# Softmax denominators of an attention stage moved from VectorE to GpSimd

## The chip, the core and the metric

The kernel runs on one core of a Trainium2 chip. Its engines are TensorE (PE in the profile; its weight loads are shown as PEld), VectorE (DVE), ScalarE (ACT), GpSimd (POOL) and SyncE (SP, which issues nearly all DMAs here). Each engine works through its own queue in program order and waits on semaphores for the others. The metric is the time of one execution on the device, in microseconds, as the median of several runs.

## The reference

Three networks follow one another. Chunked attention on q, k and v of 4 x 8 x 576 x 64 (chunks of 64 rows), then a mixture of 8 experts on 2304 x 512 whose shares are made doubly stochastic by 8 Sinkhorn rounds, then a dense layer with a softmax-gated activation and a layer norm.

```python
scores = scale * np.matmul(q_c, k_c.transpose(0, 1, 2, 4, 3))
scores = scores - np.max(scores, axis=-1, keepdims=True)
attn = np.exp(scores)
attn = attn / (np.sum(attn, axis=-1, keepdims=True) + 1e-09)   # the change is here
out = np.matmul(attn, v_c)
...
logits = x @ w_gate
P = np.exp(logits - logits.max())
for _ in range(8):
    P /= P.sum(1, keepdims=True) + 1e-09
    P /= P.sum(0, keepdims=True) + 1e-09
    P *= N / E
for e in range(E):
    h = np.maximum(x @ w1[e], 0.0)
    out += P[:, e:e + 1] * (h @ w2[e])
...
ln = (solu - mu) / np.sqrt(var + 1e-06) * g_ln
return ln @ w_out
```

## The kernel before, in words

The order of all instructions is written out by hand (a manual schedule), and every engine keeps to it.

**Attention.** 2304 rows are 18 tiles of 128 (two chunks of 64 rows each); a tile holds all 8 heads. A loop over s = 0 to 23 runs five stages of different tiles in each step, in this order: `attn_exp(s - 3)`, `attn_pv(s - 6)`, `attn_pt(s - 5)`, `attn_qk(s - 2)`, `attn_t(s)`. `attn_t` transposes q or k on PE (L196) and copies the result (ACT L201, DVE L203). `attn_qk` makes the scores (PE L214), their maxima (DVE L227) and subtracts them (DVE L228) into a tile `p` of 128x512. `attn_exp` exponentiates `p` on ACT (L240), sums each head on DVE (L241) into `sm`, 128x8, adds 1e-9 (DVE L242), takes the reciprocal (DVE L243), and multiplies `p` by it on GpSimd (L244). `attn_pt` transposes the multiplied `p` on PE (L252) two steps later, and ACT copies it (L256). `attn_pv` multiplies by v (PE L267) and copies to `xf` (ACT L279, DVE L281).

**What is woven into the same steps.** Every three tiles make a half pass of x. For the products in three passes x and the weights are split in a rounded high part (ACT, L297 for x, L150 for weights) and a low part (`split`: L151, `x_lo`: L301), and the low parts are GpSimd's here. For a Strassen-like scheme sums of blocks of x (`x_sums`, L332) and of weights (L543 to L548) are made, also on GpSimd. `run_side` and `run_w` pop such pieces from two queues once in a step, behind the attention stages. Low parts of x that are needed again later are stored to DRAM by SP (L303), and the buffer is then free for another block. From s = 18 on the first products of the experts (`l1`) are run in the steps, and for each half pass the gate's products (`gate`, PE L352), whose logits go into the Sinkhorn rounds (L380 to L421).

**After attention.** The Sinkhorn steps run beside the first expert's products; from about 200 us on the kernel is a long sequence of expert products (L663, L803, L854), and the last layer follows with a power of -0.5 on GpSimd (L1051) in each of its 18 tiles.

The change touches `attn_exp` (L237 to L246) and two places where constants are made (L140 and L1098).

Of the kernel before, what the change touches and what calls it, by code (L numbers as in the profile page):

```python
# [9 lines left out]
F32 = mybir.dt.float32  # L10
# [3 lines left out]
ALU = mybir.AluOpType  # L14
# [30 lines left out]
def chunk_attention_sinkhorn_moe_solu_kernel(  # L45
# [13 lines left out]
    nc = tc.nc  # L59
    P = 128  # L60
# [11 lines left out]
    EPS = 1e-9  # L72
# [30 lines left out]
    const = ctx.enter_context(tc.tile_pool(name="const", bufs=1))  # L103
# [34 lines left out]
    ident = const.tile([P, P], F32, name="ident")  # L138
    ones = const.tile([P, P], F32, name="ones")
    mhalf = const.tile([P, 1], F32, name="mhalf")  # L140
    g_sb = const.tile([P, KF], F32, name="g_sb")
    wg_raw = const.tile([P, KD, E], F32, name="wg_raw")

# [92 lines left out]
    def attn_exp(t):  # L236
        p, sm = attn[t]  # L237
        flat = p.rearrange("p a h x -> p (a h x)")
        heads = p.rearrange("p a h x -> p (a h) x")
        nc.scalar.activation(out=flat, in_=flat, func=AF.Exp, scale=SCALE)  # L240
        nc.vector.tensor_reduce(out=sm, in_=heads, axis=AX.X, op=ALU.add)  # L241
        nc.vector.tensor_scalar(out=sm, in0=sm, scalar1=EPS, scalar2=None, op0=ALU.add)  # L242
        nc.vector.reciprocal(out=sm, in_=sm)  # L243
        nc.gpsimd.tensor_tensor(  # L244
            out=heads, in0=heads, in1=sm.unsqueeze(2).to_broadcast([P, H, 64]), op=ALU.mult
        )  # L246
# [844 lines left out]
    with tc.manual_schedule():  # L1091
# [4 lines left out]
            nc.tensor.transpose(warm[:, :P], ident, ident)  # L1096
        nc.gpsimd.memset(ones, 1.0)
        nc.gpsimd.memset(mhalf, -0.5)  # L1098
        nc.gpsimd.memset(wg.bitcast(F32), 0.0)

        def split_gate():
# [45 lines left out]
        for s in range(NT + 6):  # L1147
# [20 lines left out]
            if 0 <= s - 3 < NT:  # L1168
                attn_exp(s - 3)
# [190 lines left out]
```

## Time and profile before

| | us |
|---|---|
| median of 3 runs | 1817.55 (1816.68 to 1820.86) |
| the profiled execution, its own time | 1817.96 |
| its span, first to last instruction | 1816.2 |
| PE busy | 1761.7 |
| DVE busy | 1468.2 |
| GpSimd busy | 1050.5 |
| ACT busy | 612.7 |

The rows of the profile name a line of the kernel (L244), an engine, an operation, the tile written and the tiles read (`p<-p,sm`, without buffer numbers), and the shape as partitions x elements. Times are counted from the start of the span. An idle time in square brackets stands in front of an instruction, with what ended it. A line can be a helper's: L151 and L301 are the low parts of many tiles. Where instructions of one engine overlap a little in the timeline, the next one had begun while the last was draining.

### The profile page before, as it was taken

What the parts mean: (1) busy time and instruction counts of PE and PEld (TensorE: products, weight loads), DVE (VectorE), ACT (ScalarE), POOL (GpSimd) and SP (SyncE); (2) the same over time, 40 slices, a digit from 0 to 9 for tenths busy, and PEclk for the clock granted to TensorE, in tenths of its full rate; (3) what the DMA queues carried; (4) which work ended last, traced back from release to release, by engine and by line L of the source; (5) the groups of instructions that cost most, each with busy time, mean ns of one, the idle gap of its engine ahead of it and who ended that gap; (6) DMA issues with size and microseconds to landing.
All of it is one profiled execution on the core that took longest, in us unless ns stands there. A gap on an engine that the chain in (4) does not pass through costs nothing.

```text
span 1816.2 us, 31895 instructions
## 1 busy us (share of the span) xinstructions
PE 1761.7 (97%) x10827; PEld 1701.4 (94%) x10827; DVE 1468.2 (81%) x2264; ACT 612.7 (34%) x1368; POOL 1050.5 (58%) x1111
## 2 busy tenths in 40 slices
PE   6889999999999999999999999999999999999999
PEld 5678999999999999999999999899999999988887
DVE  6858899999888867778788888988888877766664
ACT  6743344444444312222232222222222322222222
POOL 3776799999988415445466666566565666400000
PEclk9999999999999999999999999999999999999999
DMA  7684887988978897998987989888889878842110
GB/s 187 186 292 173 283 280 289 335 317 290 316 280 312 312 346 276 336 351 307 326 300 263 313 280 389 294 283 280 280 285 286 270 255 278 293 148 64 56 47 30
DMA packets 313443, 476.21 MB, mean 262 GB/s; under 512 B 47664, under 2 KB 116416, under 8 KB 313280
## 3 DMA queue, kind: packets, MB, share of 16 engines
q1 hardware_dynamic: 312848, 471.80, 76.0%
q8 instruction: 87, 1.43, 0.3%
q10 hardware_dynamic: 432, 2.36, 0.3%
q14 instruction: 76, 0.62, 0.1%
HBM read 323.51 MB, written 150.54 MB: 261 GB/s over the span
## 4 chain that ended last, share of the span: by engine, by line
PE 79%; DMA 5%; DVE 5%; issue 2%; POOL 1%; SPq 0%; ACT 0%; POOLq 0%; DVEq 0%; ACTq 0%
PE y L803 18%; PE y L854 17%; PE Y L663 14%; PE X L663 9%; PE Z L663 9%; PE po L1077 5%; PE mh L1020 5%; DMA wl_A<-wk 3%; PE lt L1065 1%; DMA wk<-w_S 1%; DMA x_B<-xk_B 1%; DVE acc L830 1%; DVE c L733 0%; POOL w_A L151 0%; DVE h L738 0%
## 5 line engine op out<-in xcount | busy, mean ns | idle before, releaser
L803 PE MATMUL y<-h,w_A 128*128 128x384 f32 x1536 | 305.7, 336 | 6.9 <-DVE acc L830 3.9
L683 POOL TENSOR_TENSOR ho_T<-hT,ho_T 128x384 fp32r<-128x384 f32 x188 | 210.6, 1122 | 174.4 <-ACT ho_T L682 166.9
L803 PEld LDWEIGHTS y<-h,w_A 128*128 128x128 f32 x1536 | 269.9, 188 | 10.1 <-ACT w_S L609 3.2
L151 POOL TENSOR_TENSOR w_A<-raw,w_A 128x256 fp32r<-128x256 f32 x224 | 191.7, 869 | 73.5 <-ACT w_A L150 51.1
L758 DVE TENSOR_TENSOR t<-Y,s 128x384 f32<-128x384 f32 x192 | 106.1, 552 | 112.7 <-PE Y L663 95.7
L830 DVE TENSOR_TENSOR acc<-y,acc 128x768 f32<-128x768 f32 (+1 forms) x192 | 175.6, 915 | 9.5 <-PE y L803 8.5
L854 PE MATMUL y<-ho_T,wl_S 128*128 128x384 f32 x864 | 172.8, 335 | 0.9 <-DVE acc L872 0.5
L874 DVE TENSOR_TENSOR acc<-y,acc 128x768 f32<-128x768 f32 (+1 forms) x165 | 150.5, 915 | 17.9 <-PE y L854 17.9
L803 PE MATMUL y<-h,wl_A 128*128 128x384 f32 x768 | 153.7, 337 | 3.3 <-DMA wl_A<-wk 3.3
L663 PE MATMUL Y<-x_T,wl_S 128*128 128x384 f32 x768 | 153.8, 334 | 0.0
L663 PE MATMUL X<-x_B,wl_A 128*128 128x384 f32 x768 | 153.7, 334 | 0.0
L854 PEld LDWEIGHTS y<-ho_T,wl_S 128*128 128x128 f32 x864 | 151.6, 188 | 2.1 <-DVE acc L872 0.8
L737 ACT ACTIVATE h<-c 128x384 fp32r<-128x384 f32 x132 | 69.2, 525 | 237.0 <-DVE c L733 228.4
L803 PEld LDWEIGHTS y<-h,wl_A 128*128 128x128 f32 x768 | 136.0, 190 | 4.8 <-ACT w_S L609 1.8
L682 ACT ACTIVATE ho_T<-hT 128x384 fp32r<-128x384 f32 x192 | 99.0, 516 | 108.4 <-POOL hT L691 103.5
L682 ACT ACTIVATE ho_B<-c 128x384 fp32r<-128x384 f32 x96 | 50.5, 526 | 251.7 <-DVE c L716 206.9
L663 PEld LDWEIGHTS Y<-x_T,wl_S 128*128 128x128 f32 x768 | 135.0, 188 | 0.0
L663 PEld LDWEIGHTS X<-x_B,wl_A 128*128 128x128 f32 x768 | 135.0, 188 | 0.0
L1051 POOL TENSOR_TENSOR r<-r,mhalf 128x1 f32<-128x1 f32 x18 | 9.9, 550 | 208.3 <-DVE r L1048 208.3
L758 DVE TENSOR_TENSOR c<-Z,t 128x384 f32<-128x384 f32 x192 | 105.0, 547 | 19.6 <-PE Z L663 12.7
L151 POOL TENSOR_TENSOR w_S<-ws,w_S 128x256 fp32r<-128x256 f32 x128 | 110.3, 880 | 9.3 <-ACT w_S L150 8.2
L854 PE MATMUL y<-ho_B,wl_A 128*128 128x384 f32 x576 | 114.8, 334 | 0.0
(172 smaller groups left out, 3871.6 us busy)
## 6 DMA issues: line engine op xcount, KB each, us to landing
wl_S<-wk SPq DMA_DIRECT2D x448, 256.0 KB, 5.2
wl_A<-wk SPq DMA_DIRECT2D x400, 256.0 KB, 5.2
wk<-w_S SPq DMA_DIRECT2D x256, 256.0 KB, 5.1
wk<-w_A SPq DMA_DIRECT2D x208, 256.0 KB, 4.4
raw<-in_moe_w_dram SPq DMA_DIRECT2D x77, 512.0 KB, 5.9
sh<-spread SPq DMA_DIRECT2D x64, 192.0 KB, 8.1
kept<-wp SPq DMA_DIRECT2D x32, 256.0 KB, 4.6
xk_T<-x_T SPq DMA_DIRECT2D x8, 768.0 KB, 4.8
```

Source lines behind the costliest of these rows:

```text
L151: (eng or nc.vector).tensor_tensor(out=lo, in0=src, in1=hi.bitcast(F32), op=ALU.subtract)
L663: nc.tensor.matmul(b, w[:, a, kk, :], x[:, c, kk, :], start=(first and kk == 0 and n == 0), stop=(kk == 1 and n == 2), skip_group_check=no ...
L682: nc.scalar.activation(out=hi, in_=x, func=AF.Copy)
L683: f = lambda: eng.tensor_tensor(out=lo, in0=x, in1=hi.bitcast(F32), op=ALU.subtract)
L737: nc.scalar.activation(out=hi, in_=hp, func=AF.Copy)
L758: nc.vector.tensor_tensor(out=c_of[n], in0=bank_, in1=c_of[other], op=ALU.add)
L803: nc.tensor.matmul(y, wo2[u, f"A{d // 2 + 1}{f + 1}"][:, a, i * P:(i + 1) * P], h[:, c, f, :], start=(f == 0 and n == 0), stop=(f == 1 and ...
L830: nc.vector.tensor_tensor(out=at, in0=y, in1=at, op=ALU.add)
L854: nc.tensor.matmul(y, wo2[unit(m + q_)[1], wn][:, a, i * P:(i + 1) * P], hop[m // 2, bn][:, q_, c, :], start=(q_ == 0 and o == 0), stop=(q ...
L874: nc.vector.tensor_tensor(out=at, in0=y, in1=at, op=ALU.add)
L1020: nc.tensor.matmul(ph[:, n * 512:(n + 1) * 512], x[a][:, kk, :], m_in[kk, c][:, n * 512:(n + 1) * 512], start=(kk == 0 and i == 0), stop=( ...
L1077: nc.tensor.matmul(po[t], lt[f // 4][a][:, f % 4, :], m_out[f, c], start=(f == 0 and i == 0), stop=(f == KF - 1 and i == 2),)
```

## The change

The addition of 1e-9 and the reciprocal, both on DVE, become an addition and a power of -1 on GpSimd, ahead of the multiplication that was already there. The power takes its exponent from a constant tile of 128x8, filled once at the start by GpSimd.

```diff
@@ -138,6 +138,7 @@
     ident = const.tile([P, P], F32, name="ident")
     ones = const.tile([P, P], F32, name="ones")
     mhalf = const.tile([P, 1], F32, name="mhalf")
+    mone = const.tile([P, 8], F32, name="mone")
     g_sb = const.tile([P, KF], F32, name="g_sb")
     wg_raw = const.tile([P, KD, E], F32, name="wg_raw")
 
@@ -239,8 +240,8 @@
         heads = p.rearrange("p a h x -> p (a h) x")
         nc.scalar.activation(out=flat, in_=flat, func=AF.Exp, scale=SCALE)
         nc.vector.tensor_reduce(out=sm, in_=heads, axis=AX.X, op=ALU.add)
-        nc.vector.tensor_scalar(out=sm, in0=sm, scalar1=EPS, scalar2=None, op0=ALU.add)
-        nc.vector.reciprocal(out=sm, in_=sm)
+        nc.gpsimd.tensor_scalar(out=sm, in0=sm, scalar1=EPS, scalar2=None, op0=ALU.add)
+        nc.gpsimd.tensor_tensor(out=sm, in0=sm, in1=mone, op=ALU.pow)
         nc.gpsimd.tensor_tensor(
             out=heads, in0=heads, in1=sm.unsqueeze(2).to_broadcast([P, H, 64]), op=ALU.mult
         )
@@ -1096,6 +1097,7 @@
             nc.tensor.transpose(warm[:, :P], ident, ident)
         nc.gpsimd.memset(ones, 1.0)
         nc.gpsimd.memset(mhalf, -0.5)
+        nc.gpsimd.memset(mone, -1.0)
         nc.gpsimd.memset(wg.bitcast(F32), 0.0)
```

## Rows read from the trace of the kernel before

**Rows 1.** The page, section 1: busy us, share of the span, instructions.

```profile
PE 1761.7 (97%) x10827; PEld 1701.4 (94%) x10827; DVE 1468.2 (81%) x2264; ACT 612.7 (34%) x1368; POOL 1050.5 (58%) x1111
```

**Rows 2.** Busy by stretch: us, PE, PEld, DVE, ACT, POOL busy, PEclk, DMA, GB/s.

```profile
14.00:56.08 42.08, 33.06 (x587) 28.04 (x587) 35.08 (x65) 28.44 (x51) 17.19 (x17) 0.88 0.70 168
56.08:106.65 50.57, 40.18 (x719) 34.44 (x717) 42.37 (x71) 38.48 (x70) 44.70 (x36) 0.97 0.71 204
106.65:200.00 93.35, 81.82 (x474) 76.17 (x470) 66.48 (x156) 33.88 (x88) 59.31 (x78) 0.96 0.67 240
200.00:1816.20 1616.20, 1597.39 (x8948) 1554.94 (x8947) 1319.64 (x1969) 504.49 (x1150) 928.18 (x972) 1.00 0.77 268
```

**Rows 3.** Grouped lines, 0 to 190 us: count | busy us, mean ns | idle before.

```profile
L244 POOL TENSOR_TENSOR p<-p,sm 128x512 f32<-128x512 f32 x18 | 18.8, 1042 | 31.0 <-DVE sm L243 17.8 <-ACT kt L201 13.1
...
L241 DVE TENSOR_REDUCE sm<-p 128x8 f32<-128x512 f32 x18 | 12.3, 686 | 7.9 <-ACT p L240 7.6
...
L242 DVE TENSOR_SCALAR sm<-sm 128x8 f32<-128x8 f32 x18 | 9.6, 532 | 0.6
...
L243 DVE RECIPROCAL sm<-sm 128x8 f32<-128x8 f32 x18 | 3.6, 203 | 0.6
```

**Rows 4.** Instructions of tile sm: duration ns min/median/max, first and last start.

```profile
L242 DVE TENSOR_SCALAR sm<-sm x18: 171/208/1648, 14.2 to 99.6; 128x8 f32<-128x8 f32 x18
```

**Rows 5.** Timeline, DVE and GpSimd near 58 us: start us, us.

```profile
56.08 3.59 POOL L301 TENSOR_TENSOR x_B<-xf,x_B 128x768 fp32r<-128x768 f32 x2 [1.37 <-ACT x_B L297]
...
58.38 1.31 DVE L242 TENSOR_SCALAR sm<-sm 128x8 f32<-128x8 f32 x1
```

**Rows 6.** Grouped lines of DVE, 56.08 to 102 us.

```profile
L242 DVE TENSOR_SCALAR sm<-sm 128x8 f32<-128x8 f32 x9 | 7.4, 822 | 0.3
```

**Rows 7.** Busy by stretch, GpSimd alone: us, POOL busy, PEclk, DMA, GB/s.

```profile
56.08:82.42 26.34, 26.26 (x20) 0.94 0.76 209
82.42:106.65 24.23, 18.44 (x17) 1.00 0.65 199
```

**Rows 8.** Instructions of line 1051, in the last layer.

```profile
L1051 POOL TENSOR_TENSOR r<-r,mhalf x18: 549/549/554, 1608.3 to 1802.1; 128x1 f32<-128x1 f32 x18
```

**Rows 9.** Grouped lines of GpSimd, 56.08 to 106.6 us.

```profile
L301 POOL TENSOR_TENSOR x_B<-xf,x_B 128x768 fp32r<-128x768 f32 x8 | 14.5, 1824 | 3.9 <-ACT x_B L297 3.7 <-DMA v<-in_v_dram 0.2
...
L151 POOL TENSOR_TENSOR w_S<-ws,w_S 128x256 fp32r<-128x256 f32 x4 | 2.9, 722 | 0.0
```

**Rows 10.** Timeline: two GpSimd sums, the second reading the first's result.

```profile
94.77 0.74 POOL L543 TENSOR_TENSOR ws<-raw,raw 128x256 f32<-128x256 f32 x1
...
95.58 0.74 POOL L544 TENSOR_TENSOR ws<-ws,raw 128x256 f32<-128x256 f32 x1
```

**Rows 11.** Timeline, 73 to 88 us: GpSimd's results and who uses them.

```profile
73.68 1.81 POOL L332 TENSOR_TENSOR xs_T<-xf 128x768 f32<-128x768 f32 x1
...
75.82 1.58 ACT L297 ACTIVATE x_T<-xs_T 128x768 fp32r<-128x768 f32 x2
...
81.39 1.03 POOL L244 TENSOR_TENSOR p<-p,sm 128x512 f32<-128x512 f32 x1
...
87.64 0.66 PE L252 MATMUL pt<-ident,p 128*128 128x128 f32 x4
```

**Rows 12.** Timeline, 103 to 117 us: the last splits on GpSimd and what follows.

```profile
103.03 3.62 POOL L301 TENSOR_TENSOR x_B<-xf,x_B 128x768 fp32r<-128x768 f32 x2 [0.15 <-DMA v<-in_v_dram]
...
105.54 1.47 SPq L303 DMA_DIRECT2D xk_B<-x_B  x2
...
107.19 1.64 PE L352 MATMUL pg<-x_B,wg 128*128 128x384 f32 x8
...
113.62 0.85 ACT L297 ACTIVATE x_B<-xf 128x768 fp32r<-128x768 f32 x1 [2.04 <-DMA xk_B<-x_B]
...
115.44 0.84 ACT L297 ACTIVATE x_B<-xf 128x768 fp32r<-128x768 f32 x1 [0.97 <-DMA xk_B<-x_B]
...
116.64 0.61 PE L803 MATMUL y<-h,w_A 128*128 128x384 f32 x2 [2.08 <-ACT w_A L150]
```

## The prediction, made before the changed kernel was run

> **What bounds the kernel now.** I read the page's busy line first [rows 1]: PE has work in 97% of the span, so time can be won or lost only where PE stands still. The table by stretch [rows 2] says where: from 200 us to the end PE is busy 1597.4 of 1616.2 us, while from 14 to 56.08 us it has 33.1 of 42.1, from 56.08 to 106.65 us 40.2 of 50.6, and from 106.65 to 200 us 81.8 of 93.4. The change touches only attention, whose 18 tiles run in the first two of these stretches. What follows is a fixed sequence of products on an in-order PE, so a shift of attention's end goes to the end of the kernel nearly whole. The question is what paces attention from 56.08 to 106.65 us. There DVE is busy 42.4 of 50.6 us and GpSimd 44.7, ACT 38.5 [rows 2]. DVE and GpSimd are both near their limit, and the change moves work from one to the other.
>
> **What DVE is rid of.** The grouped lines [rows 3] give per tile the sum L241 0.69 us, the addition L242 0.53 us in the mean, the reciprocal L243 0.20 us, and on GpSimd the multiplication L244 1.04 us. The addition's own work is 0.17 us, its shortest; the longest took 1.65 us [rows 4]. The long ones are waits inside the instruction: the addition that starts at 58.38 us lasts 1.31 us, to 59.69 us, and GpSimd's pair of splits that starts at 56.08 us and lasts 3.59 us ends at 59.67 us [rows 5]. So this addition stands until GpSimd's running instruction is over. In the 18 tiles that is 9.6 - 18 x 0.17 = 6.5 us [rows 3, 4], of which 7.4 - 9 x 0.17 = 5.9 us lie in the nine tiles after 56.08 us [rows 6]. With both instructions gone DVE saves 0.17 + 0.20 and two gaps of some 0.03 us, about 0.44 us a tile, or 8 us, and 6.5 us of waiting: 14.5 us in all. That is a ceiling for a gain, reached only if DVE alone paced the stage.
>
> **What GpSimd gets.** Each tile's multiplication is preceded by an addition and a power on 128x8, and both must be through before it. GpSimd runs in order, so behind them stand, in this stage, the splits of x and of the weights and the sums of x. Before 56.08 us GpSimd has 24.9 us free of 42.1 [rows 2], and most of the additional work disappears there. After it there is no room: from 56.08 to 82.42 us GpSimd is busy 26.26 of 26.34 us, and from 82.42 to 106.65 us 18.44 of 24.23 us [rows 7]. It has 0.08 + 5.79 = 5.9 us free in the whole stretch.
>
> The power's price is the unknown. The only row is the same operation on one column, 0.549 us, without spread [rows 8]. A simple instruction costs less: a split of 256 columns takes 0.722 us and one of 768 columns 1.824 us [rows 9], so 2.15 ns a column and 0.17 us for the instruction. Of the power's 0.549 us some 0.38 us are therefore its own, and the trace doesn't say whether they come once or with every column. Once: 0.55 + 7 x 0.002, about 0.56 us for eight columns. With every column: 0.17 + 8 x 0.38 = 3.2 us. Below 0.55 us it can't come, eight columns being no less work than one. I take 1.3 us, the geometric middle, which is nearer to the row: that is about a quarter of the 0.38 us for each further column. The addition is 0.17 + 8 x 0.00215 = 0.19 us. Then an instruction that needs the one before it starts late: 94.77 + 0.74 = 95.51 us, and the next at 95.58 us [rows 10], 0.07 us; there are two such links, 0.14 us. (The new memset at the start is one small instruction where GpSimd only waits for the first sums: nothing.) So a tile costs GpSimd 0.19 + 0.14 + 1.3 = 1.63 us more, 0.88 us at the low end and 3.53 us at the high end.
>
> GpSimd's row for the one column can be set beside a rule. The Trainium skill, "GPSIMD Engine Reference", section 4.1 "Engine selection", says not to put ordinary elementwise work on this engine, about twice as slow as VectorE for two inputs and about line rate for one. By it an estimate of the power would be 2 x 0.203 = 0.41 us, the tile's sum 0.74 us and the shift below 9 x 0.74 - 7.4 = -0.7 us, no change. The row of 0.549 us for a single column is already dearer, so I don't take it.
>
> **The sum.** In the stretch after 56.08 us lie nine tiles: 9 x 1.63 = 14.7 us more for GpSimd. Its 5.9 us of free time take some of it, since the late engine finds its inputs ready. And the stretch can begin earlier, by what DVE's relief before 56.08 us makes of it: nothing at least, 9 x 0.44 + 0.6 = 4.6 us at most; I take 1.5 us, since DVE is busy only 35.1 of 42.1 us there [rows 2] and the loads of q, k and v also set the pace. GpSimd's last split of the stretch then ends 14.7 - 5.9 - 1.5 = 7.3 us later than at 106.65 us.
>
> Is this lateness covered? A tile's multiplication is consumed two steps later: the one that ends at 82.42 us by the transposes at 87.64 us [rows 11], some 5 us of slack. That hides the first tiles. But GpSimd's delay is 1.63 us more with every tile, and by the fifth it is past the slack. ACT is caught sooner: the sum of x that ends on GpSimd at 73.68 + 1.81 = 75.49 us is copied by ACT at 75.82 us [rows 11], 0.3 us later, and ACT is in order; three tiles lie before it, 3 x 1.63 - 1.5 = 3.4 us of delay, and the exponentials and copies of attention wait behind that copy. So DVE's relief after 56.08 us is given back, since its inputs come late.
>
> At the end of the stretch there is no slack either [rows 12]. GpSimd's two splits end at 103.03 + 3.62 = 106.65 us, and PE's gate products start at 107.19 us. The same splits are stored by SP from 105.54 us, and ACT waits for those stores at 113.62 us (2.04 us idle) and at 115.44 us. After the second it copies the weights, for which PE waits 2.08 us at 116.64 us. A split that is 7 us late makes this whole chain 7 us late, and with it the last gate, the Sinkhorn steps and the first expert's products.
>
> The profiled execution has a span of 1816.2 us and took 1817.96 us, 0.4 us above the median of 1817.55 us; its sums hold for the median as they stand. 1817.55 + 7.3 = 1824.9 us: I predict 1825 us.
>
> **The rivals.** (1) The power costs little more than for one column. At 0.56 us the tile has 0.88 us and the shift is 9 x 0.88 - 5.9 - 1.5 = 0.5 us: 1818 us, no change. It holds up to a power of about 0.9 us, where 9 x 1.23 - 7.4 = 3.7 us. For it speaks that columns of simple instructions are cheap [rows 9]; against it that 0.38 us for a single column is more than any fixed cost that the rows show. The rule of the Trainium skill named above ends here too.
>
> (2) DVE paces the stage and GpSimd's lateness stays within the two steps of slack. Then its 14.5 us come off, until ACT, busy 38.5 of 50.6 us, is the next limit: I put half, 7 us, so 1810.5 us. It decides where the tile's additional cost on GpSimd falls below what its free time and the earlier start give, (5.9 + 1.5) / 9 = 0.8 us a tile. With the low end of the one and the ceiling of the other it is 9 x 0.88 - 5.9 - 4.6 = -2.6 us; the 7 us need, besides, that the late splits and sums are not what the stage waits for. For it speak the 5.9 us of waiting in the addition; against it that GpSimd has no free time from 56.08 to 82.42 us [rows 7].
>
> (3) The power is paid with every column, 3.2 us. Then GpSimd is full from the first tile on: 17.19 + 44.70 us [rows 2] and 18 x 3.53 = 63.5 us make 125.4 us in a stretch of 92.65 us, 32.8 us more: 1850 us.
>
> **How the numbers follow.** The forecast, a power between 0.9 and about 2.6 us, has 0.55; (3) and its neighbourhood 0.10; (1), together with a lateness that is made good after 106.65 us, where GpSimd has 34 us free [rows 2], 0.25; (2) 0.10. A measurement of this kernel can tell 0.2%, 3.6 us, from no change. So slower has 0.65, the same 0.25, faster 0.10. The range leaves out most of (2) and the far end of (3): 1815 to 1846 us. At a power of 2.6 us the shift is 9 x 2.93 - 7.4 = 19 us, so the forecast's own range is 1821 to 1837 us.
>
> **What would show it.** On the profile after: the duration of the power on 128x8, between 0.56 and 3.2 us, is the step on which all hangs. DVE should have lost both instructions, and the 6.5 us of waiting with them. GpSimd should be busy without a gap from about 55 us to the last split of attention, and that split should end some 7 us after 106.65 us, with ACT waiting for GpSimd's sums of x and PE for the multiplied tiles, where before neither did. The gap between that split and the start of the steady products should stay. I am wrong if GpSimd still has gaps in that stretch, if the transposes come earlier in spite of a later GpSimd, or if a late split is made good before 200 us.

## The result, and the profile after

The changed kernel takes 1830.76 us (median of 4 runs, 1829.84 to 1831.3) beside 1819.2 us of the kernel before (4 runs, 1816.68 to 1821.8): ratio 1.0073, interval 1.0056 to 1.0091. The two medians lie 11.6 us apart, and by the ratio it is about 13 us slower. Its profiled execution has a span of 1829.0 us, 12.8 us more than before. Nearly all of it, 12.1 us, has arisen by the end of the Sinkhorn rounds. The page's busy line of after, to be set beside [rows 1]:

```profile
PE 1767.0 (97%) x10827; PEld 1706.4 (93%) x10827; DVE 1458.2 (80%) x2228; ACT 613.5 (34%) x1368; POOL 1085.0 (59%) x1148
```

GpSimd has 34.5 us more, and 18 tiles times the two new instructions are 18 x (0.243 + 1.667) = 34.4 us. These are their durations (instructions of tile sm in after: duration ns min/median/max, first and last start):

```profile
L243 POOL TENSOR_SCALAR sm<-sm x18: 238/243/245, 16.1 to 116.8; 128x8 f32<-128x8 f32 x18
L244 POOL TENSOR_TENSOR sm<-sm,mone x18: 1665/1667/1682, 16.5 to 117.1; 128x8 f32<-128x8 f32 x18
L245 POOL TENSOR_TENSOR p<-p,sm x18: 1041/1042/1044, 18.2 to 118.8; 128x512 f32<-128x512 f32 x18
```

On DVE the reciprocal of the same 128x8 took 0.203 us [rows 3]: here the move made an operation eight times as long. The Trainium skill, "GPSIMD Engine Reference", section 4.1 "Engine selection", puts an elementwise addition, multiplication or maximum of two inputs at about twice VectorE's time there; the section names no power. The trace shows that it can't be carried over to one: the power took 1.667 us, where twice the DVE row of the reciprocal is 0.41 us.

The table by stretch of after (us, then busy time of PE, PEld, DVE, ACT, POOL, PEclk, DMA, GB/s), to be set beside [rows 2]:

```profile
14.00:56.08 42.08, 34.19 (x588) 28.26 (x584) 31.61 (x47) 30.03 (x53) 31.41 (x32) 0.89 0.73 168
56.08:106.65 50.57, 35.39 (x651) 30.12 (x650) 30.88 (x47) 33.65 (x60) 48.60 (x42) 0.90 0.61 175
106.65:120.00 13.35, 7.50 (x58) 6.20 (x58) 1.18 (x3) 4.15 (x9) 12.78 (x14) 0.74 0.48 146
```

In the second row DVE, ACT and PE all do less than before in the same 50.57 us (30.88, 33.65 and 35.39 us; before 42.37, 38.48 and 40.18), and GpSimd alone is full. From 106.65 to 120 us DVE has 1.18 us of work and GpSimd 12.78 of 13.35. PE's granted clock is lower as well, 0.90 in the second row instead of 0.97, but that can't have made GpSimd late, for GpSimd never stood for PE there. Its timeline shows it, with the stretch's first pair of splits, one tile, and the last pair:

```profile
38.54 0.73 POOL L544 TENSOR_TENSOR ws<-raw,raw 128x256 f32<-128x256 f32 x1 [3.60 <-DMA v<-in_v_dram]
...
59.15 3.60 POOL L302 TENSOR_TENSOR x_B<-xf,x_B 128x768 fp32r<-128x768 f32 x2
62.70 0.74 POOL L152 TENSOR_TENSOR w_S<-ws,w_S 128x256 fp32r<-128x256 f32 x1
63.53 0.24 POOL L243 TENSOR_SCALAR sm<-sm 128x8 f32<-128x8 f32 x1
63.85 1.67 POOL L244 TENSOR_TENSOR sm<-sm,mone 128x8 f32<-128x8 f32 x1
65.60 1.04 POOL L245 TENSOR_TENSOR p<-p,sm 128x512 f32<-128x512 f32 x1
...
119.85 3.62 POOL L302 TENSOR_TENSOR x_B<-xf,x_B 128x768 fp32r<-128x768 f32 x2
```

None of its lines from 38.54 to 119.85 us carries a bracket, those left out here included, except the first: no idle time of note. From the start of the addition to the start of the multiplication it is 65.60 - 63.53 = 2.07 us (2.08 in most tiles). The first pair begins at 59.15 us where before it was 56.08 us [rows 5], the last at 119.85 us where it was 103.03 us [rows 12]. So the stretch is 60.70 us instead of 46.95 us, 13.75 us longer, and it began 3.07 us later.

What waited for GpSimd, directly or behind another engine, from 56 to 118 us of after (engine, line and releaser: us in total, times, longest):

```profile
PE px L268 <- ACT qt L202: 9.6, 3, 4.5
PE pg L353 <- POOL x_B L302: 6.1, 2, 5.5
PE pt L253 <- POOL p L245: 2.8, 3, 1.7
...
ACT lt L361 <- PE pg L353: 11.2, 3, 8.3
ACT x_T L298 <- POOL xs_T L333: 9.9, 4, 4.3
...
DVE sm L242 <- ACT p L241: 16.1, 6, 6.3
```

PE's waits for splits and multiplied tiles, and ACT's for sums of x, are new. ACT stands 9.9 us for the sums, and 11.2 us for the gate's products (before, 4.1 us), 8.3 us of them in one piece behind the 5.5 us for which PE stands for a split. Behind ACT DVE stands for the exponentials, 16.1 us: more than the addition, its waiting and the reciprocal had cost it. At the end DVE stands for the last multiplied tile itself (waits of after from 118 us on; this one had begun earlier):

```profile
DVE xf L282 <- POOL p L245: 12.3, 1, 12.3
```

The lateness goes on to the end of attention (timeline of SP: the DMA that spreads the Sinkhorn result, first of before, then of after):

```profile
176.76 0.87 SPq L444 DMA_DIRECT2D spread<-pws  x2
```

```profile
188.89 0.88 SPq L445 DMA_DIRECT2D spread<-pws  x2
```

It comes 12.1 us later, and the last layer's first product comes at 1604.85 instead of 1592.04 us, 12.8 us later. So 16.8 us at the last split are 12.1 us at the spread, and what is late there stays late.

### The profile page after: what moved, and what is told of

It is laid out like the page before. It is cut to its first block, busy times and chain, and to the rows that moved or that the text cites. A ratio compares the mean times of both kernels' runs of the same rounds, so it can differ in the third digit from the quotient of the medians.

```text
span 1829.0 us, 31896 instructions
## 1 busy us (share of the span) xinstructions
PE 1767.0 (97%) x10827; PEld 1706.4 (93%) x10827; DVE 1458.2 (80%) x2228; ACT 613.5 (34%) x1368; POOL 1085.0 (59%) x1148
## 4 chain that ended last, share of the span: by engine, by line
PE 80%; DVE 5%; DMA 4%; POOL 2%; issue 2%; SPq 0%; ACT 0%; POOLq 0%; DVEq 0%; ACTq 0%
PE y L804 18%; PE y L855 18%; PE Y L664 15%; PE X L664 10%; PE Z L664 9%; PE po L1078 5%; PE mh L1021 5%; DMA wl_A<-wk 2%; DMA wk<-w_S 1%; PE lt L1066 1%; DMA kept<-wp 1%; POOL w_A L152 1%; DVE c L734 1%; DVE acc L831 0%; DVE h L739 0%
## 5 line engine op out<-in xcount | busy, mean ns | idle before, releaser
L875 DVE TENSOR_TENSOR acc<-y,acc 128x768 f32<-128x768 f32 (+1 forms) x165 | 150.5, 915 | 17.6 <-PE y L855 17.6
L759 DVE TENSOR_TENSOR c<-Z,t 128x384 f32<-128x384 f32 x192 | 105.2, 548 | 21.8 <-PE Z L664 14.5
```

The source lines that it names most:

```text
L759: nc.vector.tensor_tensor(out=c_of[n], in0=bank_, in1=c_of[other], op=ALU.add)
L875: nc.vector.tensor_tensor(out=at, in0=y, in1=at, op=ALU.add)
```

## The experiments

Theory Q: GpSimd's queue. The additional work delays everything behind it on GpSimd, tile after tile, so the loss grows with the price of a tile once GpSimd's free time is used up. Theory L: latency. Each tile's own chain has become longer, and what counts is the time from the sums to the multiplied tile. Rival D: DVE paces attention, so relieving it is worth something when GpSimd isn't loaded in exchange.

**One column of the power instead of eight** (seven eighths of the reciprocals are left out):

```diff
-        nc.gpsimd.tensor_tensor(out=sm, in0=sm, in1=mone, op=ALU.pow)
+        nc.gpsimd.tensor_tensor(out=sm[:, :1], in0=sm[:, :1], in1=mone[:, :1], op=ALU.pow)
```

> The changed kernel with the power on one of the eight columns (the other seven heads keep the plain sum, so 7/8 of the reciprocals are left out). Theory Q (the queue: GpSimd has no free time and all its later work, the sums and splits of x above all, is late by what each tile costs it more): the start of the addition to the start of the multiplication falls from 2.08 us to about 0.95 us a tile; GpSimd ran without a gap for 13 tiles, so its last split of attention comes 13 x 1.13 = 14.7 us earlier than in the changed kernel, and most of the 13 us come back: 1817 to 1821 us. Theory L (the latency: the multiplied tile is late for its own transposes, whatever the queue does): the tile's own chain is 1.1 us shorter, three tiles had waited for it, so 3 us come back: 1827 us.

Measured: 1823.62 us beside 1820.72 us, ratio 1.0014 (0.9999 to 1.0029). With 1.1 us less per tile, some 10 of the 13 us come back. The power took 570 ns. This stands between the two expectations, nearer to Q: the two small instructions that are left, 0.24 + 0.57 us and two links of 0.08 us, still cost a tile 0.98 us, which nine times over is a little more than GpSimd's free time.

**The power made twice**, first into a tile that nobody reads:

```diff
+        nc.gpsimd.tensor_tensor(out=again, in0=sm, in1=mone, op=ALU.pow)
         nc.gpsimd.tensor_tensor(out=sm, in0=sm, in1=mone, op=ALU.pow)
```

> The changed kernel with each power made twice, the first into a tile that nothing reads. Theory Q: every tile costs GpSimd 1.75 us more, 31.5 us in 18 tiles; it had 6.8 us of gaps before the sixth tile in the changed kernel, the rest is lateness: 24.7 us at the last split of attention, 1851 to 1856 us. Theory L: only the tiles that wait get 1.75 us more, three waits, 5 us: 1836 us.

Measured: 1854.18 us (2 runs), ratio 1.0184 (1.0156 to 1.0211). That is Q's value and out of L's reach. GpSimd's timeline in this kernel (first and last pair of splits):

```profile
67.58 3.60 POOL L304 TENSOR_TENSOR x_B<-xf,x_B 128x768 fp32r<-128x768 f32 x2
...
143.78 3.61 POOL L304 TENSOR_TENSOR x_B<-xf,x_B 128x768 fp32r<-128x768 f32 x2
```

The stretch is 76.20 us. Now the sum of theory Q can be tested with measured prices: 46.95 us of before, plus nine times a tile's price, less the 5.9 us that GpSimd had free [rows 7]. A tile's price is the time from the start of the addition to the start of the multiplication, and 0.1 us more, because the addition begins 0.09 us after its predecessor has ended (62.70 + 0.74 = 63.44, 63.53 us in the lines of after) where instructions that follow each other otherwise overlap by some hundredths.

| kernel | price of a tile, us | stretch by the sum, us | stretch measured, us | spread, us | spread later than before, us |
|---|---|---|---|---|---|
| before | 0 | | 46.95 | 176.76 | |
| one column | 0.98 + 0.1 | 50.8 | 51.37 | 180.39 | 3.6 |
| after | 2.08 + 0.1 | 60.7 | 60.70 | 188.89 | 12.1 |
| after, a second time | 2.08 + 0.1 | 60.7 | 60.69 | 186.89 | 10.1 |
| power twice | 3.79 + 0.1 | 76.1 | 76.20 | 212.62 | 35.9 |

The 0.1 us was read in after; the other two sizes test it. Where GpSimd is full the sum is right within 0.1 us. With one column it isn't quite full (0.36 us idle ahead of one pair), and the stretch is 0.6 us over the sum. The last two columns compare single profiles, and the spread of one and the same kernel differs by some 2 us from one to the next.

**The change once more**, without an edit, to have its size with more runs:

> The changed kernel as it is, beside more runs of the kernel before than its first timing had (4 and 4). By the first timing 1.0073, 1.0056 to 1.0091; by all runs of the kernel before in the later jobs (about 1820.5 us) nearer to the lower end, 1.005 to 1.007.

Measured: 1831.52 us (6 runs) beside 1819.0 us (23 runs), ratio 1.0070 (1.0055 to 1.0085). The stretch has the same length, but begins at 56.99 us, only 0.9 us later than before.

**The price of a power by itself**, on unread tiles at the start of the kernel before:

```diff
+        for i, n in enumerate((1, 2, 4, 8, 16)):
+            nc.gpsimd.tensor_tensor(
+                out=scratch[:, i * 16:i * 16 + n], in0=ones[:, :n], in1=ones[:, n:2 * n],
+                op=ALU.pow,
+            )
+        nc.gpsimd.tensor_tensor(
+            out=scratch[:, 80:88], in0=ones[:, :8], in1=ones[:, 8:16], op=ALU.mult
+        )
```

> The kernel before with six additional GpSimd instructions at the start, where GpSimd waits 13 us for the first sums: powers on 1, 2, 4, 8 and 16 columns and a product on 8, all into a tile that nothing reads. The price of a power by its columns: the two known are 0.549 us for one and 1.667 us for eight. If each further column costs the same, 0.16 us: 0.71, 1.03, 1.67 and 2.95 us; if columns go in groups, the same for 2 and 4 or for 8 and 16. The product, by the rows of the splits, 0.19 us. No change of the time.

Grouped lines of GpSimd in this kernel, 0 to 14 us (count | busy us, mean ns | idle):

```profile
L1102 POOL TENSOR_TENSOR scratch<-ones 128x16 f32<-128x16 f32 x1 | 2.9, 2902 | 0.0
L1102 POOL TENSOR_TENSOR scratch<-ones 128x8 f32<-128x8 f32 x1 | 1.6, 1637 | 0.0
L1102 POOL TENSOR_TENSOR scratch<-ones 128x4 f32<-128x4 f32 x1 | 1.0, 1014 | 0.0
L1102 POOL TENSOR_TENSOR scratch<-ones 128x2 f32<-128x2 f32 x1 | 0.7, 710 | 0.0
L1102 POOL TENSOR_TENSOR scratch<-ones 128x1 f32<-128x1 f32 x1 | 0.6, 558 | 0.0
...
L1106 POOL TENSOR_TENSOR scratch<-ones 128x8 f32<-128x8 f32 x1 | 0.2, 205 | 0.0
```

The power costs 0.40 us for the instruction and 0.156 us for every column: (2902 - 558) / 15 = 156 ns, and 558 + 7 x 156 = 1650 ns for eight, measured 1637. A product of the same shape takes 205 ns. The kernel's time, 1817.69 us beside 1820.14 us (0.9988, 0.9977 to 0.9999), shows that work on GpSimd costs nothing where it has nothing to do. In all else this is the kernel before, so its profile is a second one of it: the stretch begins at 56.78 us and is 46.91 us long, where it was 46.95, and the spread begins at 175.20 us instead of 176.76. The length of the stretch repeats within 0.1 us, the spread within 1.6 us.

**DVE relieved, GpSimd not loaded**: the kernel before without the addition (1e-9 is left out of the denominators, which are 1 at least), the reciprocal still on DVE:

```diff
-        nc.vector.tensor_scalar(out=sm, in0=sm, scalar1=EPS, scalar2=None, op0=ALU.add)
         nc.vector.reciprocal(out=sm, in_=sm)
```

> The kernel before without the addition of 1e-9 to the sums (left out; a sum of exponentials that holds an exp(0) is at least 1, where 1e-9 is lost in float32); the reciprocal stays on DVE. It measures what DVE's relief alone is worth: 18 x 0.2 us of work and 6.5 us of waiting for GpSimd inside the addition. Rival D (DVE paces attention): up to 10 us come off, 1809 us. Theory Q (GpSimd paces it from 56 to 82 us, where it has no gap): only an earlier start of that stretch and its 5.9 us of gaps after it can be won, 2 to 5 us: 1814 to 1817 us.

Measured: 1820.65 us beside 1820.72 us, ratio 1.0000 (0.9988 to 1.0011). Both expectations missed: the relief is worth nothing. From 14 to 107 us DVE is busy 77.80 us in before and 67.96 us here, 9.8 us less, about what the addition took [rows 3]. Where they went is seen in DVE's waits in that window, first of before, then of this kernel:

```profile
DVE sm L241 <- ACT p L240: 7.6, 9, 2.1
DVE xf L281 <- ACT xf L279: 4.2, 1, 4.2
```

```profile
DVE sm L241 <- ACT p L240: 13.6, 11, 2.4
DVE xf L280 <- POOL x_B L300: 4.5, 1, 4.5
DVE xf L280 <- ACT xf L278: 3.1, 1, 3.1
```

Together 11.8 us before and 21.2 us now: 9.4 us more of waiting for 9.8 us less of work. In a window of fixed length the two must nearly match; what the lines add is that DVE stood for ACT and GpSimd, and nothing behind it came earlier: the spread begins at 176.68 us, before at 176.76. GpSimd's stretch was 2.5 us shorter (59.55 to 103.95 us), but began 3.5 us later. Of this 1.8 us are the first sum of weights, at 38.62 instead of 36.85 us behind a load of v, and SP's eight loads of v that follow ran from 39.87 to 46.71 us, where before they ran from 38.32 to 44.17. Whether the edit made the loads late is not shown: in the two profiles of the changed kernel that sum stands at 38.54 and at 36.08 us.

**GpSimd relieved in the changed kernel**, by the sums of x and their low parts on DVE (14.5 us of GpSimd's work, eight instructions of 1.81 us):

```diff
-                a = x_sums(0, eng, six)
+                a = x_sums(0, nc.vector, six)
```

> The changed kernel with the sums of x and their low parts (eight instructions of 1.81 us on GpSimd, between the denominators of tiles 9 to 13) on DVE instead, some 0.95 us each there. The denominators and their price stay as they are. Theory Q: GpSimd has 14.5 us less in front of its last splits, which come about that much earlier, and DVE's 7.6 us fit in its idle time of 19.7 us between 56 and 107 us; most of the loss comes back, 1818 to 1822 us. Theory L: a tile's chain from its sum to its multiplication is as long as before, little comes back: 1828 to 1831 us.

Measured: 1825.69 us, ratio 1.0033 (1.0019 to 1.0048). About half of the loss comes back, which lies between the two expectations. The last pair of splits begins at 111.72 us, 8.1 us earlier than in after instead of 14.5 us. The rest is lost in two ways, as DVE's and GpSimd's timeline of this kernel shows:

```profile
60.93 1.75 DVE L333 TENSOR_TENSOR xs_T<-xf,xf 128x768 f32<-128x768 f32 x1
61.83 1.44 POOL L152 TENSOR_TENSOR w_S<-ws,w_S 128x256 fp32r<-128x256 f32 x1
...
73.58 0.94 DVE L333 TENSOR_TENSOR xs_T<-xf,xs_T 128x768 f32<-128x768 f32 x1
73.91 2.39 POOL L245 TENSOR_TENSOR p<-p,sm 128x512 f32<-128x512 f32 x1
74.44 0.95 DVE L333 TENSOR_TENSOR xs_T<-xf 128x768 f32<-128x768 f32 x1
...
83.09 0.24 POOL L243 TENSOR_SCALAR sm<-sm 128x8 f32<-128x8 f32 x1 [1.50 <-DVE sm L242]
```

A sum that takes DVE 0.95 us takes 1.75 us beside GpSimd's splits, a split of 0.73 us takes 1.44 us beside such sums, and GpSimd's multiplication 2.39 instead of 1.04 us beside two sums. On GpSimd the longer instructions add up to some 3.5 us in the stretch. And GpSimd now has gaps of 3.6 us, 2.0 us for DVE's sums, of which the last line shows 1.50 us, and 1.6 us for a copy of ACT.

**The last splits on DVE in the changed kernel** (of the fourth and fifth half pass; the sixth was there already):

```diff
-            eng = nc.vector if hp == NT // TH - 1 else nc.gpsimd
+            eng = nc.vector if hp >= NT // TH - 3 else nc.gpsimd
```

> The changed kernel with the splits of x of the fourth and fifth half pass on DVE (four instructions of 1.8 us on GpSimd, between the denominators of tiles 15, 16, 17 and behind them), which is idle there. In the changed kernel PE waits 5.5 us at 114.7 us for the second of them. Theory Q: that wait goes, GpSimd's queue is 3.6 us shorter before the multiplication of tile 16's successor, and PE reaches the gate's products of the fifth half pass some 6 us earlier: 5 to 7 us off the changed kernel, a ratio to the kernel before of 1.003 to 1.005. Theory L: only the wait for these splits itself, and the tiles' waits then take its place: 1.006 to 1.008.

Measured: 1830.32 us, ratio 1.0055 (1.0040 to 1.0070), hardly anything, between the two expectations. PE's wait of 5.49 us for a split in after is gone, and another stands in its place. The timeline of PE in after, then in this kernel:

```profile
114.69 1.33 PE L353 MATMUL pg<-x_B,wg 128*128 128x384 f32 x3 [5.49 <-POOL x_B L302]
```

```profile
118.60 1.11 PE L253 MATMUL pt<-ident,p 128*128 128x128 f32 x4 [3.24 <-POOL p L245]
```

The multiplication of the last tile still ends at 118.54 us, against 119.89 us in after, since it stands behind 18 powers on the same engine, and GpSimd's instructions are again longer beside DVE's splits (a pair of splits 4.30 instead of 3.60 us, with three others 2.9 us in all, of the 3.6 us that were taken out ahead of that tile). So not one late split, but everything that GpSimd still had to do was late.

**Can what the change was after be had otherwise?** Four kernels on the kernel before, all without the addition: with the sums of x on DVE, with the loads of v issued ahead of those of q and k, this together with the splits of the fifth half pass on DVE, and all of it. The edit for the sums is the one shown above, that for the splits has `NT // TH - 2`; the loads are moved by:

```diff
+            if 0 <= s - 2 < NT:
+                load_v(s - 2)
             if s % 2 == 0 and s + AHEAD < NT:
                 load_qk((s + AHEAD) // 2)
-            if 0 <= s - 2 < NT:
-                load_v(s - 2)
```

> The kernel before without the addition (left out) and with the eight sums and low parts of x on DVE. GpSimd's stretch without a gap from 56 to 82 us is 14.5 us shorter, DVE has lost 10 us and gains 8 to 10 us. If GpSimd paced attention before the change, 3 to 8 us come off: a ratio of 0.996 to 0.998. If the loads of v and PE's own order pace it, none: 0.999 to 1.002.

> The kernel before without the addition (left out) and with the loads of v issued ahead of those of q and k in each step. In the run without the addition PE waited 3.8 us at 46.5 us for a load of v that SP had issued behind q and k. If that wait is what takes DVE's relief back, it goes, and 2 to 4 us come off: a ratio of 0.998 to 0.999. If not, or if q and k are then late, none or a loss: 1.000 to 1.003.

> The kernel before without the addition (left out), the loads of v ahead of those of q and k, and the two splits of x of the fifth half pass on DVE, which is idle there. Those splits, and the stores behind them, are what ACT, and PE behind it, wait for at the end of attention in the kernel before. If this chain and the load of v are what attention's end hangs on, 3 to 5 us come off: a ratio of 0.997 to 0.9985. If the later stages make up for it, none.

> As the run before it, with the eight sums and low parts of x on DVE as well: GpSimd has 14.5 us less in the stretch where it had no gap. If GpSimd's queue paces attention as soon as the loads of v are early, 5 to 8 us come off: 0.9955 to 0.997. If DVE, now with these eight instructions and contending with GpSimd, paces it instead, the same as the run before it or worse.

Measured, in this order: 1.0003 (0.9988 to 1.0017), 0.9997 (0.9985 to 1.0010), 1.0015 (1.0001 to 1.0029) and 1.0004 (0.9994 to 1.0015). No gain in any. The wait of 3.8 us at 46.5 us, which the second expectation puts down to a load of v, is put down by the profile to DVE's reciprocal, and no row names the load there; with v first these products of PE with v start at 42.39 us, after a wait of 0.60 us. With v first the last pair of splits begins at 98.48 us, 4.5 us earlier than before, but the timeline of ACT and PE in that kernel shows the next limit:

```profile
110.11 0.84 ACT L296 ACTIVATE x_B<-xf 128x768 fp32r<-128x768 f32 x1 [3.46 <-DMA xk_B<-x_B]
112.69 0.84 ACT L296 ACTIVATE x_B<-xf 128x768 fp32r<-128x768 f32 x1 [1.74 <-DMA xk_B<-x_B]
113.89 1.01 PE L802 MATMUL y<-h,w_A 128*128 128x384 f32 x2 [4.28 <-ACT w_A L150]
```

ACT waits 5.2 us for the stores of x, where it was 3.0 us [rows 12], and PE 4.28 us instead of 2.08 us. In this profile the spread still begins 2.8 us earlier than before (174.00 us), and with all reliefs 3.3 us earlier (173.43 us), with the sums on DVE 2.0 us earlier (174.75 us), and with v first and the splits on DVE 1.4 us later (178.19 us); in the medians nothing of that remains. Why, is not settled: single profiles of one kernel differ by 2.0 us at the spread (the changed one) and by 1.6 us (the one before), so most of this may lie within what one execution differs from the next. It would fit an end of attention in the kernel before at which several chains of nearly the same length meet, of GpSimd, DVE, the loads and the stores; that is not shown. No relief here beats it.

## Why the prediction was right, and where its steps were off

The forecast was 1825 us, slower, by a GpSimd that is late from the middle of attention on. The time is 1830.76 us, slower by more than the forecast and within its own range of 1821 to 1837 us. The forecast was a shift of 7.3 us from a median of 1817.55 us; the measured shift is 11.6 us between the medians, 12.5 us with more runs and 12.8 us between the profiles. That the mechanism is this one is shown by the stretch, which follows the price of a tile in three sizes.

- **The power**, taken at 1.3 us between 0.56 and 3.2 us, is 1.667 us, and the addition 0.243 instead of 0.19 us. The middle of the bounds was a quarter of 0.38 us for each further column, 0.1 us; it is 0.156 us. The two links are 0.08 us each, taken as 0.07 from [rows 10]. A third was not counted: the addition's own late start, 0.1 us. Together a tile costs 2.2 us instead of 1.63 us, nine times 0.55 us: 5 us.
- **GpSimd's free time of 5.9 us** [rows 7] is right: it is the 5.9 us of the table's sum.
- **The start of the stretch** was the step that failed. It was put 1.5 us earlier, by DVE's relief, and GpSimd's own additional work ahead of it at nothing, because GpSimd has 24.9 us free before 56.08 us; it came 3.07 us later. Of that free time 17.6 us lie before 36.85 us, where GpSimd waits for a tile's reciprocals and for loads. Between 36.85 and 56.08 us, the table by stretch of before (us, POOL busy, PEclk, DMA, GB/s) has:

```profile
36.85:56.08 19.23, 11.97 (x12) 0.91 0.71 176
```

  So 7.3 us are free there, and four tiles bring 4 x 2.2 = 8.8 us. That makes 1.5 us of lateness by itself; from the first sum of weights to the stretch it is 20.61 us in after instead of 19.23, 1.4 us more, and 1.7 us more in the second profile of the change. The other 1.7 us are that first sum itself, at 38.54 instead of 36.85 us behind loads; in the second profile it stands at 36.08 us, and the stretch begins 0.9 us late. In either case late, not early. Free time must be read where the work falls, not over a whole stretch.
- **"A split that is 7 us late makes this whole chain 7 us late"** was too strong. The last pair is 16.8 us late and the spread 12.1 us, so 4.7 us were made good before 200 us, in part what the prediction had named as a sign of being wrong; 4.5 us in the second profile, 4.2 us with one column, 4.9 us with the power twice. The timelines show where. The gate's products behind the last pair, at 107.19 us before [rows 12], come at 122.89 us, while the pair still runs: 15.7 us late, 1.1 us made good. Then, before, ACT stood 2.04 and 0.97 us for the stores of x, and PE 2.08 us behind it [rows 12]. In after the same copies read:

```profile
128.13 1.58 ACT L298 ACTIVATE x_B<-xf 128x768 fp32r<-128x768 f32 x2 [0.81 <-DVE xf L282]
```

They wait for no store any more, and the copies of weights behind them, at 116.19 us before and 129.62 us in after, are 13.4 us late: another 2.3 us. But the wait for the stores is not a fixed part of the kernel before. In its second profile, that of the kernel with the prices, the same copies read:

```profile
113.06 1.58 ACT L298 ACTIVATE x_B<-xf 128x768 fp32r<-128x768 f32 x2 [0.81 <-DVE xf L282]
```

Set beside that profile the last pair is 16.2 us late and the spread 13.7 us, so only 2.5 us are made good. The last 1.4 us come mostly with the last gate's products (PE, first of before, then of after):

```profile
120.14 2.76 PE L352 MATMUL pg<-x_B,wg 128*128 128x384 f32 x8
```

```profile
133.35 1.55 PE L353 MATMUL pg<-x_B,wg 128*128 128x384 f32 x8
```

The granted clock was 0.50 during the first (the lower level, 1.2 GHz; PE had stood 2.08, 0.66 and 0.30 us ahead of it) and 1.00 during the second (2.4 GHz; 0.79 and 0.54 us). In the second profile of before it is 0.50 too, behind waits as short as those of after, so the waits alone don't explain it. So the prediction had read as part of the path a wait for stores that one execution has and another doesn't, and had left out the slack at the gate and the clock.

- **The sum**, with the measured sizes: 7.3 + 5.0 + 4.6 = 16.9 us at the last split, where 16.8 us are measured. Of these the spread shows 12.1 us, 4.7 us less. The start put too early (4.6 us) and the lateness believed to stay (4.7 us) cancel each other by luck, so the forecast came out closer than its steps; what remained is the price of a tile, 5.0 us.
- **ACT waiting for sums of x and PE for multiplied tiles** came as foretold, 9.9 and 2.8 us. The largest wait of PE for GpSimd, 5.49 us for a split, had been expected only at the end of the stretch. The waiting inside the addition, 6.5 us, is gone with it, and bought nothing.

Of the rivals, (1) falls with the power's 1.667 us, which is over its bound of 0.9 us; the kernel with one column, at 0.57 us, is what it would have looked like, 1.0014. (3) falls too: the columns do cost, but 0.156 us each and not 0.38 us. (2), DVE as the pacer, had been given 7 us; the kernel without the addition has the larger part of that relief, at no cost for GpSimd, and gains 0.0 us.

## What to carry to other kernels

Before work is moved to an engine, read how much of its time is free in the very stretch where the work will stand, and what stands behind it in that queue: here 2.2 us a tile against 5.9 us of gaps made a stretch 13.75 us longer, as a plain sum of measured prices gives it to a tenth of a microsecond. An operation's price on another engine should be measured on the shape in question, since one column of a power said little about eight. And busy time taken from an engine that doesn't set the pace is worth nothing: 9.8 us less on DVE, with GpSimd not loaded for it, left the time where it was (1.0000).

## What the hardware showed that was not expected

- A power on GpSimd is paid by the column: 0.558 us for one, 2.902 us for sixteen, 0.156 us each, while a product of eight columns takes 0.205 us in all.
- DVE and GpSimd lengthen each other, and not only where DVE runs the small addition of [rows 5]. A sum on DVE took 1.75 us instead of 0.95 us beside GpSimd's splits, and GpSimd's multiplication took 2.39 us instead of 1.04 us beside DVE's sums. The Trainium skill, "SBUF — State Buffer", section "Who interferes with whom", says that a DVE instruction with two inputs in SBUF contends with a GpSimd instruction that reads SBUF, and that whichever comes first blocks the other. The trace agrees that each of them can be the one that is held up. So of the 14.5 us of work that were moved from a full GpSimd to DVE some 3.5 us came back as longer instructions on GpSimd, and only 8.1 us were won at the last splits.
